# Clustered attention and a rational MoE layer on one core: the denominator's constant moves to ScalarE in three quarters of the units, under a new written-out order

## The chip, the core and the metric

The kernel runs on one core of a Trainium2 chip. The core has TensorE (PE in the profile), VectorE (DVE), ScalarE (ACT) and GpSimd (POOL) as compute engines and SyncE (SP), which issues the transfers here. Each engine works through its own list of instructions in order; between engines only semaphores order anything. The metric is the device time of one execution in microseconds (us), lower is better.

## What is computed

The reference, cut to what matters:

```python
# q, k, v: (4, 8, 768, 64); centroids: (8, 16, 64); w_in: (512, 2048); w_out: (2048, 512)
q_assign = argmax(einsum('bhsd,hcd->bhsc', q_n, c_n))      # the nearest of 16 centroids
k_assign = argmax(einsum('bhsd,hcd->bhsc', k_n, c_n))
mask = q_assign[:, :, :, None] == k_assign[:, :, None, :]
scores = where(mask, scale * q @ k^T, -1e9)
attn = exp(scores - max); attn = attn / (sum(attn) + 1e-9)
x = (attn @ v), heads put side by side: 3072 tokens x 512
h = x @ w_in
P = a[0] + a[1] * h + a[2] * h**2 + a[3] * h**3
Q = 1.0 + abs(b[0]) * abs(h) + abs(b[1]) * h**2
g = P / (Q + 1e-06)
out = g @ w_out
```

## The kernel before

The work is a batch's attention (four batches, four head pairs each), and behind it the batch's share of the MoE layer. The parts overlap: while the MoE of one batch runs, the attention of the next does. All products are made of float16 high and low parts, so a matrix product is three or four matmul passes.

**Attention.** For a head pair and a block of 128 queries, TensorE makes a tile of scores `s` (L987, four matmuls per head into one of two PSUM buffers named "s"). VectorE scales it and takes the extreme (L1016), ScalarE does the exponential and, with a tiny Copy, the sum's scale (`su`); VectorE inverts the sum (L1035); ScalarE writes the normalised high part `ah`, VectorE the low part (L1047), which is the last reader of the PSUM buffer. Then SP transposes `ah` to `at`, and TensorE multiplies by V (`px`, L1067). A batch-0 variant with keys first has lines from L1111 to L1225. L390 is the line of a helper through which nearly all ScalarE instructions go, so the names of the tiles tell them apart.

**MoE.** The work falls into 96 units: 4 batches x 3 blocks of 256 tokens x 4 blocks of the 2048 inner columns (`ci`) x 2 halves (`h`). A unit is a tile of 128 x 512. TensorE makes `ph` (the h of the reference; L1274, 24 matmuls, into one of two PSUM buffers named "m"); ScalarE reads it into `u` (absolute value) and `t` (start of the cubic); VectorE carries the cubic on (L1291, L1292, the last readers of `ph`). GpSimd completes the square of the denominator (L1336, L1337: s = u * (u + constant), so that Q = s + `cq`). ScalarE takes Ln of Q and Exp of its negative, which makes `u` about 1/Q. Then s becomes (s + cq) * u, t becomes (t + a0) * u (GpSimd L1365 and L1366, or VectorE L1372), and VectorE joins them in one Newton step (L1377). ScalarE casts the result to float16 (L1381), GpSimd or VectorE makes the low part (L1385), and TensorE multiplies by `w_out` into `po` (L1396, 12 matmuls of 128 x 512 per unit, six for each of its two blocks of 128 rows).

The constant `cq` can be added in two ways, and `acq`, a share between 0 and 1 spread evenly over the units, says in which:

```python
                acq = kshare("acq", b, i_)
                if acq:
                    act((724, 1165)[k], sv, sv, AF.Identity, [], ss, uu + kb("ln", b), [s_t], bias=cq)
                act((630, 1070)[k] if acq else (724, 1165)[k], uv, sv, AF.Ln, ss, us, uu + kb("ln", b), [s_t, u_t], **({} if acq else {"bias": cq}))
```

With `acq`, ScalarE adds it once in an Identity of its own, and Ln and the product (L1359) take s as it is. Without it, Ln takes cq as its bias, and GpSimd adds cq to s once more (L1354) ahead of the product L1359. In the last batch (`ed.3` is 1) VectorE makes the product (L1348) and adds the constant in the same instruction, so there is no L1354 there, with or without `acq`; the halves h = 1 of that batch use tiles named `sq1`, `sq2` and `sk1`, so that ScalarE's rows there read sq<-sq.

**Order.** The kernel writes some 4,200 steps into a list, and ORDER, a table of numbers, says in which order they are emitted; nothing reorders them behind it. So ORDER alone sets what stands where in each engine's list. The first number of each step's call (724 and so on) is not used.

Of the kernel before, what the change touches and what calls it, by code (L numbers as in the profile page):

```python
# [9 lines left out]
F32 = mybir.dt.float32  # L10
F32R = mybir.dt.float32r
F16 = mybir.dt.float16
BF16 = mybir.dt.bfloat16
# [5 lines left out]
P = 128  # L19
# [38 lines left out]
K = {'mulp': 0.6, 'mulp.3': 0.0, 'a0t': 1.15, 'xn': 14, 'scp': 1, 'vsc': 0.75, 'sup0': 0, 'stk': 2, 'lop': 0, 'mgp': 0, 'rvn': 2, 'at': 3, 'vn': 3, 'ah': 5, 'sqd': 0.0, 'ed': 0.0, 'ed.3': 1.0, 'gld': 0.0, 'gld.3': 1.0, 'sqd.3': 0.0, 'ghd': 0.0, 'sua': 1.0, 'acq': 0.4}  # L58
# [188 lines left out]
def clustered_attention_moe_kernel(  # L247
# [82 lines left out]

    plan.look = kn("look", 40.0)
    NM = 2
    NR = kn("NR", 12)

    def misc(shape, dt, name):
        return bank(shape, dt, "m", name, NM)
# [1149 lines left out]
```

## Time and profile before

| | |
|---|---|
| median of 3 runs | 958.12 us (957.24 to 958.2) |
| the profiled execution's own time | 954.15 us |
| its span in the trace | 952.3 us |
| mean granted TensorE clock | 0.993 |
| TensorE busy | 865.9 us |
| VectorE busy | 859.5 us |
| ScalarE busy | 802.1 us |
| GpSimd busy | 765.1 us |

The span is the time from the first to the last recorded instruction of the profiled execution; the time of that execution has 1.85 us more around it. Busy is the time in which an engine had at least one instruction in work; a matmul's end is modelled, so a busy TensorE need not be at its peak.

### The profile page before, as it was taken

To read this page: it belongs to the slowest core of one execution; us is meant where nothing else is said; L and a number is where in the kernel's file an instruction comes from. 1 tells how busy PE (TensorE), PEld (TensorE's weight loads), DVE (VectorE), ACT (ScalarE), POOL (GpSimd) and SP (SyncE) were. 2 spreads that over 40 slices of the span, in tenths; PEclk is the share of its full clock that TensorE was granted. 3 is DMA by queue.
4 is the path that set the end of the run, shared out by engine and by line. 5 is a ranking of instruction groups with operands and counts; after the bars stand their busy time and mean duration, and the time that the engine had idled before them with its cause. 6 is when DMAs were issued, how large, how long until landed. Compare 5 with 4: busy or idle time off the path is not lost.

```text
span 952.3 us, 20719 instructions
## 1 busy us (share of the span) xinstructions
PE 865.9 (91%) x7705; PEld 580.6 (61%) x7705; DVE 859.5 (90%) x1522; ACT 802.1 (84%) x1524; POOL 765.1 (80%) x801
## 2 busy tenths in 40 slices
PE   1679997988999998999989999999999999999997
PEld 1347665665666665656656666575576665766763
DVE  6888899778979999999999999999999998899986
ACT  5476786999989999889899999999899898876763
POOL 3557788899989899999998999998999998254452
PEclk9979999999999999999999999999999999999999
DMA  7994866797957779696879789696977667502000
GB/s 213 236 225 128 181 170 164 179 206 163 180 100 128 158 130 219 119 174 108 170 133 180 129 146 202 119 171 105 172 152 147 97 131 142 106 2 56 1 23 22
DMA packets 358932, 132.98 MB, mean 140 GB/s; under 512 B 335280, under 2 KB 351664, under 8 KB 358832
## 3 DMA queue, kind: packets, MB, share of 16 engines
q1 hardware_dynamic: 358832, 131.67, 68.8%
q8 instruction: 60, 0.98, 0.4%
q14 instruction: 40, 0.33, 0.1%
HBM read 41.98 MB, written 6.29 MB: 51 GB/s over the span
## 4 chain that ended last, share of the span: by engine, by line
PE 37%; DVE 32%; ACT 13%; issue 8%; DMA 6%; POOL 4%; SPq 0%; ACTq 0%; DVEq 0%; POOLq 0%
PE ph L1274 13%; PE po L1396 11%; DVE s L1016 6%; DVE ah L1047 5%; PE s L987 4%; PE px L1067 3%; DVE t L1377 3%; ACT s L390 3%; DMA rwi<-in_moe_w_in_dram 3%; DVE t L1291 2%; ACT u L390 2%; ACT ah L390 2%; DVE t L1292 2%; DVE top L1120 2%; DMA sq<-tq 2%
## 5 line engine op out<-in xcount | busy, mean ns | idle before, releaser
L1274 PE MATMUL ph<-x,win 128*128 128x256 f16 x2304 | 270.6, 273 | 3.7 <-DVE t L1292 3.1
L1274 PEld LDWEIGHTS <-win 128*128 128x128 f16 x2304 | 223.9, 98 | 49.4 <-DVE t L1292 5.9
L1396 PE MATMUL po<-wout,s 128*128 128x512 f16 x1008 | 239.5, 380 | 0.9 <-POOL s L1385 0.5
L1396 PEld LDWEIGHTS <-s 128*128 128x128 f16 x1008 | 96.5, 98 | 104.5 <-issue 4.6
L1016 DVE TENSOR_SCALAR_CACHE_REDUCE s<-s,cc 128x768 f32<-128x768 f32 x144 | 145.5, 1016 | 11.7 <-PE s L987 11.0
L1047 DVE SCALAR_TENSOR_TENSOR ah<-s,su,ah 128x768 f16<-128x768 f32 x144 | 144.7, 1009 | 7.4 <-ACT ah L390 6.6
L390 ACT ACTIVATE ah<-s,su 128x768 f16<-128x768 f32 x144 | 129.0, 899 | 18.0 <-DVE su L1035 17.1
L390 ACT ACTIVATE s<-s,nm 128x768 f32<-128x768 f32 x144 | 125.7, 873 | 12.5 <-DVE s L1016 11.1
L987 PE MATMUL s<-sk,sq 128*128 128x384 f16 x576 | 116.8, 327 | 19.6 <-DVE ah L1047 17.9
L1337 POOL TENSOR_TENSOR s<-s,u 128x512 f32<-128x512 f32 x84 | 113.9, 1356 | 7.0
L1359 POOL TENSOR_TENSOR s<-s,u 128x512 f32<-128x512 f32 x72 | 98.8, 1376 | 3.3 <-ACT u L390 3.1
L1385 POOL TENSOR_TENSOR s<-t,s 128x512 f16<-128x512 f32 x72 | 88.8, 1234 | 12.4 <-ACT s L1381 12.1
L1336 POOL TENSOR_SCALAR s<-u,g 128x512 f32<-128x512 f32 x84 | 77.2, 919 | 23.0 <-ACT u L390 21.7
L1377 DVE SCALAR_TENSOR_TENSOR t<-s,t 128x512 f32<-128x512 f32 x84 | 91.6, 1090 | 2.7 <-POOL s L1359 2.4
L987 PEld LDWEIGHTS <-sq 128*128 128x128 f16 x576 | 50.4, 98 | 67.6 <-DVE ah L1047 37.2
L1067 PE MATMUL px<-at,vhi 128*64 128x256 f16 x864 | 75.8, 277 | 4.3 <-DVE t L1292 4.1
L390 ACT ACTIVATE u<-ph,gk 128x512 f32<-128x512 f32 x84 | 57.4, 684 | 15.7 <-PE ph L1274 15.5
L1292 DVE SCALAR_TENSOR_TENSOR t<-t,gk,ph 128x512 f32<-128x512 f32 x84 | 62.8, 748 | 3.0
L390 ACT ACTIVATE t<-ph,gk 128x512 f32<-128x512 f32 x84 | 65.1, 777 | 0.0
L1291 DVE SCALAR_TENSOR_TENSOR t<-ph,gk,t 128x512 f32<-128x512 f32 x84 | 62.2, 740 | 1.0 <-ACT t L390 0.7
L1067 PE MATMUL px<-at,vlo 128*64 128x256 f16 x432 | 60.7, 275 | 0.0
L1366 POOL TENSOR_TENSOR t<-t,u 128x512 f32<-128x512 f32 x43 | 56.6, 1317 | 4.1 <-ACT u L390 0.6
(225 smaller groups left out, 1773.6 us busy)
## 6 DMA issues: line engine op xcount, KB each, us to landing
rwi<-in_moe_w_in_dram SPq DMA_DIRECT2D x16, 512.0 KB, 4.5
rwo<-in_moe_w_out_dram SPq DMA_DIRECT2D x16, 512.0 KB, 4.1
rk<-in_k_dram SPq DMA_DIRECT2D x32, 192.0 KB, 3.1
rq<-in_q_dram SPq DMA_DIRECT2D x32, 192.0 KB, 3.4
rvm<-in_v_dram SPq DMA_DIRECT2D x16, 384.0 KB, 4.0
rv<-in_v_dram SPq DMA_DIRECT2D x16, 384.0 KB, 4.4
out_dram<-ob SPq DMA_DIRECT2D x24, 256.0 KB, 3.0
at<-ah SPq DMA_TRANSPOSE x144, 4.1
```

The source lines that it names most:

```text
L390: lambda: nc.scalar.activation(out=out(), in_=in_(), func=func, **{a: (x() if callable(x) else x) for a, x in kw.items()}),
L987: nc.tensor.matmul(sc.ap[:, i, :SH], lhsT=st["q" + x].ap[:, j, t, :], rhs=st["k" + x].ap[:, j, ks, :].rearrange("p t c -> p (t c)"), start ...
L1016: lambda nm=nm, view=view: ts(out=view(), in0=view(), scalar1=cc.ap[:, 0:1], scalar2=None, op0=ALU.mult, op1=ALU.min, accum_out=nm.ap),
L1047: lambda part=part, view=view, su=su: stt(out=part(1), in0=view(), scalar=su.ap, in1=part(0), op0=ALU.mult, op1=ALU.subtract),
L1067: nc.tensor.matmul(px.ap[j * D : (j + 1) * D, :], lhsT=vv.ap[:, j, kt, :], rhs=at[j].ap[:, p_, kt].rearrange("p t c -> p (t c)"), start=(i ...
L1274: nc.tensor.matmul(ph.ap[:, fi * TW : (fi + 1) * TW], lhsT=win[:, wpart, c, f * P : (f + 1) * P], rhs=xs[c].ap[:, xpart], start=(i == 0), ...
L1292: stt(out=t[h].ap, in0=t[h].ap, scalar=col("a1")(), in1=ph.ap, op0=ALU.add, op1=ALU.mult)
L1337: nc.gpsimd.tensor_tensor(out=sv(), in0=sv(), in1=uv(), op=ALU.mult)
L1359: lambda uv=uv, sv=sv: nc.gpsimd.tensor_tensor(out=sv(), in0=sv(), in1=uv(), op=ALU.mult),
L1377: lambda tv=tv, sv=sv: stt(out=tv(), in0=sv(), scalar=2.0, in1=tv(), op0=ALU.subtract, op1=ALU.mult),
L1385: lambda tv=tv, g16=g16, e=(nc.vector if kshare("gld", b, i_) else nc.gpsimd): e.tensor_tensor(out=g16(1), in0=tv(), in1=g16(0), op=ALU.su ...
L1396: nc.tensor.matmul(po[ti].ap, lhsT=g16(gg)[:, c0 : c0 + P], rhs=wout[:, wpart, f, :], start=(i == 0 and f == 0), stop=(i == 2 and f == NF ...
```

## The change

The share `acq` goes from 0.4 to 0.75, and ORDER is written anew. Over the 96 units the Identity on ScalarE is there 72 times and not 38. In the first three batches that is 54 of 72 units and not 28: 26 units lose the GpSimd addition L1354 (44 before, 18 after) and get an Identity, and their Ln loses its bias. In the last batch it is 18 of 24 and not 10: 8 units get an Identity, and there is no GpSimd addition to lose. No other engine gains or loses a compute instruction (TensorE's, VectorE's lists hold as many rows as before).

```diff
-K = {'mulp': 0.6, 'mulp.3': 0.0, 'a0t': 1.15, 'xn': 14, 'scp': 1, 'vsc': 0.75, 'sup0': 0, 'stk': 2, 'lop': 0, 'mgp': 0, 'rvn': 2, 'at': 3, 'vn': 3, 'ah': 5, 'sqd': 0.0, 'ed': 0.0, 'ed.3': 1.0, 'gld': 0.0, 'gld.3': 1.0, 'sqd.3': 0.0, 'ghd': 0.0, 'sua': 1.0, 'acq': 0.4}
+K = {'mulp': 0.6, 'mulp.3': 0.0, 'a0t': 1.15, 'xn': 14, 'scp': 1, 'vsc': 0.75, 'sup0': 0, 'stk': 2, 'lop': 0, 'mgp': 0, 'rvn': 2, 'at': 3, 'vn': 3, 'ah': 5, 'sqd': 0.0, 'ed': 0.0, 'ed.3': 1.0, 'gld': 0.0, 'gld.3': 1.0, 'sqd.3': 0.0, 'ghd': 0.0, 'sua': 1.0, 'acq': 0.75}
...
 ORDER = [int(i) for i in """
-3 376 377 28 374 4 5 375 6 7 40 8 9 379 381 10 29 382 383 32 30 388 31 391 380 34 392 44 384 41 385 489 393
...
+3 377 376 28 374 4 5 375 6 7 40 8 9 379 381 29 382 383 32 30 10 388 31 391 380 34 33 392 44 384 41 385 398 489
...
-    NR = kn("NR", 12)
+    NR = kn("NR", 12 if kn("gw", 1) == 1 else 6)
...
+    def weights_wide(name, i, vt):
...
-                weights("wi", i, kn(f"wi{i}", -24 + 2.5 * i))
-                weights("wo", i, kn(f"wo{i}", -22 + 2 * i))
+                (weights_wide if GW == 2 else weights)("wi", i, kn(f"wi{i}", -24 + 2.5 * i))
+                (weights_wide if GW == 2 else weights)("wo", i, kn(f"wo{i}", -22 + 2 * i))
```

K has neither "gw" nor "c3" in it, so GW stays 1: the new function weights_wide is never called, NR stays 12, and the edit of a claim list (`tiles[: 3 if kn("c3") else 2]`) makes the same list as before. The new function shifts the lines behind it by 121: L1354 of before is L1475 of after.

What the new order does is seen in three places.

TensorE, around 361 us of the profiled execution: the last two score tiles of head pair 2 of batch 1 (`s1_2_5_0`, `s1_2_5_1`) and the first of head pair 3 (`s1_3_0_0`), which takes the PSUM buffer of `s1_2_5_0`. The first rows of each set, before:

```order
L987 MATMUL s1_2_5_0_5086<-sk11_2_3515,sq11_2_3542 128x384
...
L987 MATMUL s1_2_5_1_5098<-sk11_2_3515,sq11_2_3542 128x384
...
L1067 MATMUL px1_2_1_5119<-at1_2_1_0_4827,vhi1_2_3795 64x256
...
L987 MATMUL s1_3_0_0_5176<-sk11_3_4354,sq11_3_4378 128x384
```

and after:

```order
L1108 MATMUL s1_2_5_0_5074<-sk11_2_3521,sq11_2_3543 128x384
...
L1517 MATMUL po0_2_5083<-wout_104,s0_2_0_0_4741 128x512
...
L1108 MATMUL s1_2_5_1_5099<-sk11_2_3521,sq11_2_3543 128x384
...
L1517 MATMUL po0_2_5083<-wout_104,s0_2_0_0_4741 128x512
...
L1188 MATMUL px1_2_1_5124<-at1_2_1_0_4809,vhi1_2_3976 64x256
...
L1108 MATMUL s1_3_0_0_5178<-sk11_3_4355,sq11_3_4409 128x384
```

Each set of `po` left out here is of 6 matmuls and that of `px` of 36, in both lists. Two sets of `po` have come in between `s1_2_5_0` and `s1_3_0_0`, where before only the other score tile and the `px` stood.

ScalarE, at the MoE's first units (batch 0, block 0, ci 0): `u0_0_0_1`, `t0_0_0_1` and `s0_0_0_1` are the tiles of the half h = 1. Before:

```order
L390 ACTIVATE ah1_0_1_1_3057<-s1_0_1_1_2955,su1_0_1_1_3004 128x768
L390 ACTIVATE u0_0_0_0_2981<-u0_0_0_0_2981 128x512
L390 ACTIVATE rvm2_3_2934,vm2_2805<-rvm2_3_2934 128x768
L390 ACTIVATE u0_0_0_1_3008<-s0_0_0_1_3050,cq_76 128x512
L390 ACTIVATE u0_0_1_0_3096<-ph0_0_1_0_3011,gk0_2320 128x512
L390 ACTIVATE u0_0_0_1_3008<-u0_0_0_1_3008 128x512
```

and after:

```order
L390 ACTIVATE s0_0_0_1_3043<-s0_0_0_1_3043,cq_76 128x512
L390 ACTIVATE ah1_0_2_0_3131<-s1_0_2_0_3037,su1_0_2_0_3083 128x768
L390 ACTIVATE u0_0_0_1_3013<-s0_0_0_1_3043 128x512
L390 ACTIVATE u0_0_1_1_3153<-ph0_0_1_1_3087,gk0_2323 128x512
L390 ACTIVATE u0_0_0_1_3013<-u0_0_0_1_3013 128x512
```

The Identity `s0_0_0_1<-s0_0_0_1,cq` is new, and the Ln behind it (`u0_0_0_1<-s0_0_0_1`) has no bias; an `ah` of the attention stands between the two.

ScalarE, at the very end: the last unit is `ph3_2_3_1`, with its tiles `sq1`, `sk1` and `sq2`. Before:

```order
L390 ACTIVATE sk13_2_3_13059<-ph3_2_3_1_13000,gk3_8995 128x512
L1381 CAST s3_2_3_0_12956<-t3_2_3_0_12966 128x512
L390 ACTIVATE sq13_2_3_13045<-sq23_2_3_13054,cq_76 128x512
L390 ACTIVATE sq13_2_3_13045<-sq13_2_3_13045 128x512
L1381 CAST sq23_2_3_13054<-sk13_2_3_13059 128x512
```

and after:

```order
L1502 CAST s3_2_3_0_12958<-t3_2_3_0_12981 128x512
L390 ACTIVATE sq23_2_3_13063<-sq23_2_3_13063,cq_76 128x512
L390 ACTIVATE sq13_2_3_13043<-sq23_2_3_13063 128x512
L390 ACTIVATE sq13_2_3_13043<-sq13_2_3_13043 128x512
L1502 CAST sq23_2_3_13063<-sk13_2_3_13046 128x512
```

The last unit is one of those that get the Identity. In TensorE's list the last `ph` of this unit is followed by 54 matmuls of `po` before and by 60 after.

Elsewhere the new order keeps the stages and their sequence (the same head pair of attention stands beside the same block of the MoE), and moves single steps by a few places. At the start of the program the load `rv0_1` (384 KB) stands ahead of the transposes of `sk2` and `sq2` of head pair 0 and not behind them, and one preparation step of `w_in` on GpSimd (L555) is earlier.

## Rows read from the trace of the kernel before

**Rows 1.** The page, part 1: busy us, share of span, instructions:
```profile
PE 865.9 (91%) x7705; PEld 580.6 (61%) x7705; DVE 859.5 (90%) x1522; ACT 802.1 (84%) x1524; POOL 765.1 (80%) x801
```

**Rows 2.** Windows: length, busy us of each engine, clock, DMA:
```profile
180.00:780.00 600.00, 565.08 (x4983) 378.85 (x4983) 560.63 (x1018) 555.92 (x1088) 558.56 (x588) 1.00 0.80 150
780.00:953.00 173.00, 165.38 (x1193) 106.55 (x1192) 149.16 (x214) 121.64 (x212) 85.31 (x70) 1.00 0.25 50
```

**Rows 3.** The page, part 4: the chain by engine and line:
```profile
PE 37%; DVE 32%; ACT 13%; issue 8%; DMA 6%; POOL 4%; SPq 0%; ACTq 0%; DVEq 0%; POOLq 0%
PE ph L1274 13%; PE po L1396 11%; DVE s L1016 6%; DVE ah L1047 5%; PE s L987 4%; PE px L1067 3%; DVE t L1377 3%; ACT s L390 3%; DMA rwi<-in_moe_w_in_dram 3%; DVE t L1291 2%; ACT u L390 2%; ACT ah L390 2%; DVE t L1292 2%; DVE top L1120 2%; DMA sq<-tq 2%
```

**Rows 4.** The view of waits: us in total, times, longest:
```profile
PEld L987 <- DVE ah L1047: 37.2, 55, 1.9
...
PE s L987 <- DVE ah L1047: 17.9, 31, 1.4
```

**Rows 5.** Groups by form, the edited instructions: busy, mean ns:
```profile
L390 ACT ACTIVATE u<-s,cq 128x512 f32<-128x512 f32 x50 | 36.1, 722 | 3.7 <-POOL s L1337 3.6
...
L1354 POOL TENSOR_SCALAR s<-s,cq 128x512 f32<-128x512 f32 x44 | 34.5, 786 | 3.9 <-ACT su L390 1.6 <-ACT u L390 1.6
...
L390 ACT ACTIVATE s<-s,cq 128x512 f32<-128x512 f32 x34 | 24.4, 717 | 6.6 <-POOL s L1337 6.6
...
L390 ACT ACTIVATE u<-s 128x512 f32<-128x512 f32 x34 | 21.3, 626 | 0.2
```

**Rows 6.** One line (L1354): min/median/max ns, first and last start:
```profile
L1354 POOL TENSOR_SCALAR s<-s,cq x44: 686/695/1230, 217.9 to 797.1; 128x512 f32<-128x512 f32 x44
```

**Rows 7.** Groups by form, VectorE in the MoE part:
```profile
L1377 DVE SCALAR_TENSOR_TENSOR t<-s,t 128x512 f32<-128x512 f32 x84 | 91.6, 1090 | 2.7 <-POOL s L1359 2.4
...
L1292 DVE SCALAR_TENSOR_TENSOR t<-t,gk,ph 128x512 f32<-128x512 f32 x84 | 62.8, 748 | 3.0
...
L1372 DVE SCALAR_TENSOR_TENSOR t<-t,gk,u 128x512 f32<-128x512 f32 x41 | 44.8, 1092 | 0.1
...
L1372 DVE SCALAR_TENSOR_TENSOR sk<-sk,gk,sq 128x512 f32<-128x512 f32 x12 | 9.1, 760 | 0.3
...
L1377 DVE SCALAR_TENSOR_TENSOR sk<-sq,sk 128x512 f32<-128x512 f32 x12 | 8.6, 720 | 0.3
```

**Rows 8.** Timeline of TensorE: start, duration, instruction, idle before:
```profile
361.32 0.81 PE L987 MATMUL s<-sk,sq 128*128 128x384 f16 x4
362.38 0.82 PE L987 MATMUL s<-sk,sq 128*128 128x384 f16 x4 [0.24 <-DVE ah L1047]
364.76 0.41 PE L1067 MATMUL px<-at,vhi 128*64 128x256 f16 x4 [1.55 <-DVE t L1292]
...
368.20 0.82 PE L987 MATMUL s<-sk,sq 128*128 128x384 f16 x4 [1.29 <-DVE ah L1047]
```

**Rows 9.** Chain from 180 to 780 us: start, us, work:
```profile
243.17 2.59 PE po L1396 x12
...
245.76 2.10 PE px L1067 x36
```

**Rows 10.** Windows, 840 to 900 us:
```profile
840.00:900.00 60.00, 59.95 (x441) 41.03 (x440) 57.42 (x76) 42.14 (x71) 28.69 (x24) 1.00 0.12 23
```

**Rows 11.** Timeline of all engines at the end:
```profile
933.40 1.47 PE L1274 MATMUL ph<-x,win 128*128 128x256 f16 x12
...
939.54 0.72 ACT L390 ACTIVATE sq<-sq,cq 128x512 f32<-128x512 f32 x1 [0.34 <-POOL sq L1337]
...
944.18 0.62 ACT L1381 CAST sq<-sk 128x512 f16<-128x512 f32 x1 [3.26 <-DVE sk L1377]
...
944.88 3.04 PE L1396 MATMUL po<-wout,sq 128*128 128x512 f16 x12
```

**Rows 12.** Windows, 220 to 240 us:
```profile
220.00:240.00 20.00, 17.84 (x142) 11.62 (x141) 17.08 (x32) 19.69 (x40) 19.00 (x17) 1.00 0.83 179
```

More of the change, by code (lines that the diff above doesn't have):

```diff
@@ L627, in weights, with high, low, squares @@
                 )
+    def weights_wide(name, i, vt):
+        ew = wie if name == "wi" else woe
+        acc = buf([P, 1], F32, "acc", f"{name}a{i}", 2)
+        junk = temp([P, P], f"{name}j{i}")
+        ws = [buf([P, GW, FW], I32, "ring", f"w{name}{i}_{q}", NR) for q in range(2)]
+        for q, w in enumerate(ws):
+            halves = [half(w, h) for h in range(2)]
+            mag = wide(f"m{name}{i}_{q}")
+            mags = [half(mag, h) for h in range(2)]
+            raws = []
+            for h in range(2):
+                c = 2 * q + h
+                n = f"{name}{i}_{c}"
+                if name == "wi":
+                    src = moe_w_in[c * P : (c + 1) * P, i * FW : (i + 1) * FW]
+                else:
+                    src = moe_w_out[(4 * i + c) * P : (4 * i + c + 1) * P, :]
+                raw = buf([P, 2 * FW], I32, "wraw", "r" + n, 2)
+                raws.append(raw)
+                dma(1460, lambda raw=raw: raw.ap, lambda src=src: src.bitcast(I32), [], [raw], vt - kn("wd", 3))
+                def high(raw=raw):
+                    return raw.ap.rearrange("p (f two) -> p two f", two=2)[:, 1, :]
+                act(
+                    668, lambda mags=mags, h=h: mags[h].ap, lambda high=high: high().bitcast(F32), AF.Copy, [raw], [mags[h]], vt, [mag],
+                    scale=2.0 ** -112,
+                )
+            dve(
+                1050,
+                lambda w=w, mag=mag: nc.vector.tensor_single_scalar(
+                    out=w.ap, in_=mag.ap.bitcast(I32), scalar=3, op=ALU.logical_shift_left
+                ),
+                mags, halves, vt, [w, mag], n=1,
+            )
+            for h, raw in enumerate(raws):
+                def low(raw=raw):
+                    return raw.ap.rearrange("p (f two) -> p two f", two=2)[:, 0, :]
+                def high(raw=raw):
+                    return raw.ap.rearrange("p (f two) -> p two f", two=2)[:, 1, :]
+                dve(
+                    930,
+                    lambda w=w, h=h, low=low: stt(
+                        out=w.ap[:, h], in0=low(), scalar=29, in1=w.ap[:, h], op0=ALU.logical_shift_right, op1=ALU.bitwise_or
+                    ),
+                    [raw], [halves[h]], vt, [w], n=1,
+                )
+                act(
+                    668, lambda mags=mags, h=h: mags[h].ap, lambda high=high: high().bitcast(F32), AF.Sign, [raw], [mags[h]], vt, [mag],
+                )
+            op(
+                "POOL", 2300,
+                lambda w=w, mag=mag: nc.gpsimd.tensor_tensor(
+                    out=w.ap.bitcast(F32), in0=w.ap.bitcast(F32), in1=mag.ap, op=ALU.mult
+                ),
+                [*mags, *halves], [w], vt, [mag],
+            )
+        gram = misc([P, P], F32, f"{name}g{i}")
+        def squares():
+            blocks = [
+                w.ap.rearrange("p h c -> p (h c)").bitcast(BF16).rearrange("p (n two) -> p two n", two=2)[:, 1, m * P : (m + 1) * P]
+                for w in ws for m in range(2 * FW // P)
+            ]
+            for m, x in enumerate(blocks):
+                nc.tensor.matmul(gram.ap, lhsT=x, rhs=x, start=(m == 0), stop=(m == len(blocks) - 1))
+        op("PE", 1640, squares, ws, [gram], vt, [acc, junk])
+        dve(
+            360,
+            lambda: stt(
+                out=junk.ap, in0=gram.ap, scalar=1.0, in1=ident, op0=ALU.mult, op1=ALU.mult, accum_out=acc.ap
+            ),
+            [gram], [acc, junk], vt,
+        )
+        pn = misc([P, 1], F32, f"{name}n{i}")
+        def total():
+            nc.tensor.matmul(pn.ap, lhsT=ones, rhs=acc.ap, start=True, stop=True)
+        op("PE", 250, total, [acc], [pn], vt)
+        s = wsc[name]
+        we = Buf(None, None, 0, False)
+        whl[name, i, "e"] = we
+        ws_ = Buf(None, None, 0, False)
+        root_pow2(
+            pn, f"{name}p{i}", vt, lambda: ew.ap[:, i : i + 1], [ew, we], lambda: s.ap[:, i : i + 1], [ws_]
+        )
+        for q, w in enumerate(ws):
+            hl = [whl[name, i, 2 * q + h] for h in range(2)]
+            def part(j, q=q):
+                if name == "wi":
+                    return win[:, j, 2 * q : 2 * q + 2, i * FW : (i + 1) * FW]
+                return wout[:, j, 4 * i + 2 * q : 4 * i + 2 * q + 2, :]
+            def wf(w=w):
+                return w.ap.bitcast(F32)
+            act(
+                1160, lambda part=part: part(0), wf, AF.Identity, [w, ws_], hl, vt,
+                scale=lambda: s.ap[:, i : i + 1],
+            )
+            op(
+                "POOL", 1240,
+                lambda wf=wf: nc.gpsimd.tensor_scalar(
+                    out=wf(), in0=wf(), scalar1=s.ap[:, i : i + 1], scalar2=0.0, op0=ALU.mult, op1=ALU.add
+                ),
+                [ws_], [w], vt,
+            )
+            op(
+                "POOL", 2100,
+                lambda part=part, wf=wf: nc.gpsimd.tensor_tensor(out=part(1), in0=wf(), in1=part(0), op=ALU.subtract),
+                [w], hl, vt,
+            )
@@ L1282, in moe @@
                 for fi in range(2):
-                    op("PE", 12 * 108, lambda fi=fi, first=first: first(fi), [*xs, *wi, *wo, gk], [ph], u_ + h + kb("ph", b), tiles[:2], chain="ph")
+                    op("PE", 12 * 108, lambda fi=fi, first=first: first(fi), [*xs, *wi, *wo, gk], [ph], u_ + h + kb("ph", b), tiles[: 3 if kn("c3") else 2], chain="ph")
                 act(688, lambda u=u, h=h: u[h].ap, lambda ph=ph: ph.ap, AF.Abs, [ph, gk], [u[h]], u_ + h + kb("phr", b), [u_t], scale=col("kap"))
```

360 rows, old and new, of the table ORDER are left out of this document.

## The prediction

> **What bounds the kernel now.** I read the busy times first. Over the whole span TensorE is busy 91%, VectorE 90%, ScalarE 84%, GpSimd 80% [rows 1]: nobody has much room, and an average over stages hides which engine sets the pace where. So the span is cut in three [rows 2]. From 180 to 780 us, where attention of one batch and MoE of another run together, the four are within ten microseconds of each other: TensorE 565.1, VectorE 560.6, GpSimd 558.6, ScalarE 555.9 of 600. The reader should see four engines at 93 to 94%, none at 100: they wait for one another in turn, and TensorE idles 600 - 565.1 = 35 us. From 780 us on it is another picture: TensorE 165.4 of 173, ScalarE only 121.6, GpSimd 85.3. There TensorE alone is the bound.
>
> The chain that ended last agrees [rows 3]: 37% TensorE, 32% VectorE, 13% ScalarE, 4% GpSimd. A microsecond of work is not worth the same on every engine. ScalarE has 0.13 x 952.3 = 124 us on the chain out of 802.1 busy, which is 0.154 us of chain for each us of work; VectorE 305 of 859.5, 0.355; GpSimd 38 of 765.1, 0.05. These shares are my exchange rates for spread-out edits. They are local (a chain bends when work is added), so each has bounds beside it.
>
> The view of waits says what TensorE waits for: scores wait for VectorE's L1047, the last reader of the PSUM buffer they need, 37.2 us in 55 places at the weight loads and 17.9 in 31 at the matmuls [rows 4]. The two sums are of two queues that overlap in part, so they exceed the 35 us that TensorE really idled.
>
> **The change, part by part.** The profiled execution took 954.15 us (span 952.3, 1.85 around it), about 4 us under the median of 958.12. The sum is made against the former and then set on the median.
>
> *ScalarE.* A unit with the Identity costs 717 (Identity) + 626 (Ln without bias) - 722 (Ln with bias) = 621 ns more [rows 5]. In the first three batches 26 units change: 26 x 0.621 = 16.1 us. At 0.154 that is **+2.5 us**. Bounds: 0, if all of it falls into ScalarE's 44 us of idle time in that stretch; +16.1, if all of it is on the path. The 8 units of the last batch cost 8 x 0.621 = 5.0 us in a stretch where ScalarE idles 51 of 173 us: nothing, but for the last unit, which is counted under the tail.
>
> *GpSimd.* 26 of the 44 instructions L1354 go, at 786 ns: 20.4 us [rows 5]. All 44 lie between 217.9 and 797.1 us [rows 6], so the relief falls into the crowded stretch and none into the last one. At 0.05 it is **-1.0 us**; bounds 0 and -20.4.
>
> *VectorE, by way of GpSimd.* The instructions of VectorE that read two operands from SBUF are slower where GpSimd is busy. L1377 takes 1090 ns in its form with t (84 of them, over all stretches) and 720 in the form with sk (12, all in the last batch); L1372 1092 (41) against 760 (12). L1292, one operand of which is in PSUM, takes 748 in the same crowded stretch [rows 7]. The excess is 84 x 0.370 + 41 x 0.332 = 44.7 us. If it goes with GpSimd's busy time, 20.4 of 765.1 us less frees 1.2 us of VectorE; if it goes with GpSimd's busy share (93.1% in the middle, 49.3% at the end [rows 2]: 370 ns for 43.8 points, and 20.4 of 600 us is 3.4 points), it frees 29 ns on 125 instructions, 3.6 us. At 0.355: -0.4 to -1.3; I take the middle, **-0.9**.
>
> The Trainium skill has a harsher rule for this pair ("SBUF — State Buffer", section "Who interferes with whom"): a VectorE instruction with two SBUF inputs contends with a GpSimd instruction that reads SBUF, and the later one waits until the earlier has ended. The stretched 1090 and the unstretched 748 agree with which instructions it concerns. By it every dropped L1354 would hand VectorE its whole length, which is the fourth rival below.
>
> *The order, scores.* Two PSUM buffers serve the scores, so TensorE can make a tile only when the tile two before has been read by L1047. At 361 us the buffer of one tile is written until 361.32 + 0.81 = 362.13 and taken again at 368.20, after 1.29 us of waiting: the way round took 6.1 us [rows 8]. In between the old order gives TensorE only the other tile (0.82) and 36 `px` (2.10 us [rows 9]), 2.9 us of work, and TensorE waited 1.55 and 1.29 there. The new order puts two sets of six `po` in, 1.30 us each [rows 9]: 5.5 us. I counted this distance for all 142 pairs of the row-wise attention in both orders, with these durations. Under 6 us: 16 pairs, 11.7 us short in total before, 13 pairs, 9.4 after. Under 5 us: 3.2 short before, 1.4 after. So 1.8 to 2.3 us of waits fall away: **-2.0**, with 0 as the other bound, where the engines ahead of L1047 are late anyhow.
>
> *The tail.* From 840 to 900 us TensorE is busy 59.95 of 60 us [rows 10], so when the last `ph` comes is set by how much TensorE has ahead of it. The new order puts six `po` matmuls behind it that stood ahead: 1.30 us earlier [rows 9]. Behind it comes a chain of one unit through ScalarE, GpSimd and VectorE, from `ph` at 933.40 to the last `po` at 944.88, with Ln at 939.54 and the cast at 944.18 [rows 11]; ScalarE has waited 3.26 us ahead of that cast, so nothing else sets it. The new Identity adds 0.62 to this chain. Net **-0.7**; bounds -1.3 and +0.6. In the first three batches the same 0.62 is hidden: this chain, 10.0 us from the end of the last `ph` (933.40 + 1.47) to 944.88, is the only one I have to measure it by, and both orders leave TensorE at least 13 us of other work between a unit's `ph` and its `po`. Where a unit had no such cover, it would cost its 0.62.
>
> *The start.* The load of V for head pair 1 moves ahead of two transposes, and one weight step moves forward. No row prices it. I take 0.
>
> Sum: 2.5 - 1.0 - 0.9 - 2.0 - 0.7 = -2.1 us. 954.15 becomes 952.0, and the median 958.1 becomes **956.0**.
>
> **The rivals.**
>
> *A, the balance above:* 956.0, its own range 951 to 961 (the Identities at twice their exchange rate, or at none; the order's terms at 0 or as they stand).
>
> *B, the order gives more than I can count.* The 35 us that TensorE idles in the middle come from many places; I counted one kind. For it: scores waiting on L1047 are the largest wait in the view [rows 4]. Against it: the milestones of the two orders are alike, and steps moved only by some places. A quarter of the 35 us, 8.8: about 949.
>
> *C, the other side: ScalarE becomes the bound.* In the middle stretch it goes from 555.9 to 572.0 us, above TensorE's 565.1. The busiest engine there now runs at 565.1 / 600 = 94.2%. If ScalarE can do no better, the stretch becomes 572.0 / 0.942 = 607 us, +7.3; with the tail's -0.7 that gives about 964.5. It decides once ScalarE has gained over 9.2 us, 15 of the 26 units. For it: behind the first MoE units ScalarE is busy 19.69 of 20 us already [rows 12], so it can be full, and everything that TensorE waits for (exponential, `ah`, `u`) goes through it. Against it: only 13% of the chain is its own, and at 19.69 of 20 it shows that it can run well above 94%.
>
> *D, the shared access is the true bound.* If each dropped L1354 hands VectorE its 695 ns [rows 6], 26 of them are 18.1 us, all of them worth it if VectorE set the pace: 940. Against it: the mean stretch is 370, not 695 ns, and VectorE has a third of the chain.
>
> *E, nothing happens:* each engine's terms are absorbed by its neighbours' idle time, 958.
>
> **How the numbers follow.** About 0.2%, 1.9 us, is what a measurement of this kernel can tell from no change. Chances: A 0.50, B 0.15, C 0.22, D 0.05, E 0.08. The point is A's 956.0, 2.1 us under the median, so A itself is split: about half of it faster by more than 1.9 us, a third within, the rest slower. Faster: 0.26 of A with B and D, 0.46. Same: 0.18 of A with E, 0.26. Slower: 0.06 of A with C, 0.28. The range, 947 to 965, takes in A and E, most of B, and the nearer half of C; it leaves out D, B's far end and C's worse half, some 2 in 10.
>
> **What the profile after would show.** L1354, now L1475, 18 times, and ScalarE's busy time near 802.1 + 16.1 + 5.0 = 823, GpSimd's near 745: else the counts are wrong. The means of L1377 and L1372 in their forms with t some 10 to 30 ns lower: if 100 or more, D is at work. Waits of scores for L1047 some 2 us less, and no 1.29 ahead of `s1_3_0_0`. At the end the last `ph` starts about 1.3 us earlier in relation to TensorE's work, and the way from there to the last `po` is 0.6 longer. If ScalarE shows over 96% from 180 to 780 us and TensorE's waits on ScalarE's tiles grow by more than those on L1047 shrink, C was right and the exchange rate of 0.154 is the step that failed. A start that is later by more than a microsecond would make the forecast wrong with none of these steps at fault.

## The result: 12.7 us faster, where 2.1 were forecast

| | before | after |
|---|---|---|
| median of 4 runs | 958.16 us | 945.46 us (943.42 to 947.64) |
| ratio | 1 | 0.9868 (95%: 0.9838 to 0.9897) |
| profiled execution, span | 954.15, 952.3 us | 947.64, 945.9 us |

The ratio's interval is a gain of 9.9 to 15.5 us. The direction was right; the size was six times too small and the time lies below the range (947 to 965). The two profiled executions differ by only 6.5 us: that of before lies under all four runs of its row and had a mean granted TensorE clock of 0.993, that of after is the slowest of its four and had 0.987. So stages are compared by work done in a stretch, not by span alone.

The page of the changed kernel, part 1 (busy us of each engine) and part 4 (the chain):

```profile
PE 868.2 (92%) x7705; PEld 584.7 (62%) x7705; DVE 857.7 (91%) x1522; ACT 814.1 (86%) x1558; POOL 743.2 (79%) x775
...
PE 42%; DVE 27%; ACT 15%; issue 8%; DMA 6%; POOL 2%; SPq 1%; ACTq 0%; DVEq 0%; POOLq 0%
```

Against [rows 1, 3] GpSimd is down by 22 us, ScalarE up by 12, TensorE and VectorE as they were: the same work in less time. VectorE's share of the chain fell from 32% to 27%, TensorE's rose from 37% to 42%. ScalarE was forecast near 823 us and shows 814.1, though it ran the 34 additional instructions. Busy time counts once what overlaps, and in this order more of ScalarE's work overlaps (see x3_identity_at_ln).

The windows of the changed kernel, columns as in [rows 2]:

```profile
180.00:780.00 600.00, 573.25 (x5065) 386.71 (x5064) 568.72 (x1030) 570.81 (x1131) 549.88 (x570) 1.00 0.80 152
780.00:946.00 166.00, 158.16 (x1123) 102.48 (x1121) 141.08 (x200) 118.76 (x205) 71.43 (x61) 0.99 0.23 46
```

In the same 600 us TensorE was busy 573.3 us and not 565.1, VectorE 568.7 and not 560.6, and ScalarE, which got the additional work, 570.8 and not 555.9. The middle of the program is denser on three engines at once; TensorE idles 26.8 us there and not 34.9. ScalarE stands at 95.1% there, above the 94.2% that I took for what an engine can reach.

The groups by form of the changed kernel, those that answer to [rows 5, 7]:

```profile
L1498 DVE SCALAR_TENSOR_TENSOR t<-s,t 128x512 f32<-128x512 f32 x84 | 85.8, 1022 | 0.1
...
L1493 DVE SCALAR_TENSOR_TENSOR t<-t,gk,u 128x512 f32<-128x512 f32 x41 | 46.4, 1131 | 0.2 <-ACT u L390 0.2
...
L390 ACT ACTIVATE s<-s,cq 128x512 f32<-128x512 f32 x60 | 43.5, 724 | 1.1 <-POOL s L1458 1.1
...
L1475 POOL TENSOR_SCALAR s<-s,cq 128x512 f32<-128x512 f32 x18 | 15.3, 850 | 0.5 <-ACT su L390 0.2
```

The counts are as forecast: 18 additions on GpSimd, 60 Identities of this form (12 more on the sq tiles). L1498, which was L1377, came down by 68 ns; L1493, which was L1372, went up by 39; together 4.1 us less VectorE work.

### The profile page after: what moved, and what is told of

Read it like the earlier page. It is cut to its first block, busy times and chain, and to the rows that moved or that the text cites. A ratio compares the mean times of both kernels' runs of the same rounds, so it can differ in the third digit from the quotient of the medians.

```text
span 945.9 us, 20726 instructions
## 1 busy us (share of the span) xinstructions
PE 868.2 (92%) x7705; PEld 584.7 (62%) x7705; DVE 857.7 (91%) x1522; ACT 814.1 (86%) x1558; POOL 743.2 (79%) x775
## 4 chain that ended last, share of the span: by engine, by line
PE 42%; DVE 27%; ACT 15%; issue 8%; DMA 6%; POOL 2%; SPq 1%; ACTq 0%; DVEq 0%; POOLq 0%
PE ph L1395 14%; PE po L1517 13%; DVE s L1137 6%; DVE ah L1168 5%; PE s L1108 5%; ACT s L390 3%; PE px L1188 3%; DVE t L1498 2%; ACT ah L390 2%; DVE t L1412 2%; DMA rwi<-in_moe_w_in_dram 2%; ACT u L390 2%; DVE t L1413 2%; PE s L1232 2%; PE z L1276 2%
## 5 line engine op out<-in xcount | busy, mean ns | idle before, releaser
L1457 POOL TENSOR_SCALAR s<-u,g 128x512 f32<-128x512 f32 x84 | 76.0, 905 | 37.3 <-ACT u L390 31.9
L1498 DVE SCALAR_TENSOR_TENSOR t<-s,t 128x512 f32<-128x512 f32 x84 | 85.8, 1022 | 0.1
```

The source lines that it names most:

```text
L1498: lambda tv=tv, sv=sv: stt(out=tv(), in0=sv(), scalar=2.0, in1=tv(), op0=ALU.subtract, op1=ALU.mult),
```

## The experiments

Times are medians; each ratio is to the kernel before in runs on the same chip, with its 95% interval. The first run below, e1_old_order_acq75, is the order of before with the share 0.75. Its order and the new one differ by 462 exchanges of neighbours (two steps that follow each other in an engine's list change places) on TensorE, 1798 on ScalarE, 1062 on VectorE, 633 on GpSimd and 566 on SP; no TensorE step moves by more than ten places.

### The edit without the order, the order without the edit

The steps that one order has and the other lacks are tied to a neighbour: an Identity directly ahead of its Ln, an addition directly ahead of its product. For the first run (`was` is the share for which the order was written):

```diff
-                if acq:
-                    act((724, 1165)[k], sv, sv, AF.Identity, [], ss, uu + kb("ln", b), [s_t], bias=cq)
+                if was:
+                    op("ACT", 724, plus if acq else (lambda: None), [], ss)
...
+                def ln(uv=uv, sv=sv, plus=plus, put=acq and not was, bias=not acq):
+                    if put:
+                        plus()
+                    nc.scalar.activation(out=uv(), in_=sv(), func=AF.Ln, **({"bias": cq} if bias else {}))
```

**e1_old_order_acq75.** 

> The order of before with the share 0.75: the Identity is put directly ahead of its Ln, the additions L1354 that the change drops are dropped, nothing else moves. If the new order made the gain (theory O: fewer waits of scores and of TensorE by where the steps stand), this is near before, 956 to 960 us. If the edit made it (theory R: GpSimd's 20 us less work and what VectorE gets back of it), this is near the changed kernel, 944 to 949. By my exchange rates (2.5 - 1.0 - 0.9 and the tail's 0.6) it would be 959.

Measured: 962.02 us, 1.0040 (1.0024 to 1.0057).

**e2_new_order_acq40.** 

> The new order with the share 0.4: the additions on GpSimd are put back directly ahead of their product, the Identities go. Theory O: near the changed kernel, 943 to 948 us. Theory R: near before, 955 to 959. If both are needed (the new order was made for the other split of work and fits only that), it is slower than both single effects would give, and the first run is slower than before too.

Measured: 953.11 us, 0.9946 (0.9927 to 0.9965), between the two theories. So:

| | order of before | new order | the order is worth |
|---|---|---|---|
| share 0.4 | 1 | 0.9946 | -5 us |
| share 0.75 | 1.0040 | 0.9868 | -16 us |
| the edit is worth | +4 us | -7 us | |

Neither theory holds alone: the edit costs time under the old order and saves time under the new one. By themselves the edit and the order make +3.8 and -5.2 us, together -1.4; with both it is -12.7. Some 11 us (7 to 15, from the three intervals) come only when the new order and the new share are together. A hint at why is in the chains (part 4 of the two pages), first of the order of before with 0.75:

```profile
PE 35%; DVE 28%; ACT 18%; issue 8%; DMA 6%; POOL 4%; SPq 0%; ACTq 0%; DVEq 0%; POOLq 0%
```

then of the new order with 0.4:

```profile
PE 33%; DVE 26%; POOL 17%; ACT 10%; issue 8%; DMA 5%; POOLq 0%; SPq 0%; ACTq 0%; DVEq 0%
```

Under the old order the Identities put ScalarE on the chain with 18%, and before it was 13% [rows 3]. Under the new order and the old share GpSimd has 17% of the chain; in the changed kernel it has 2%. So with the other split one engine takes a larger part of the chain than in either kernel. That this is the cause is argued, not shown: shares of the chain turn out below to be poor prices. And part of the 11 us may lie in where these two runs put the steps that their order lacks, directly beside a neighbour.

### The two halves of the edit, each alone

**e3_drop_adds_only** leaves out the addition L1354 in all but 18 units (the edit is given in short; `acq_new` is the share of the changed kernel, `acq_old` that of before):

```diff
-                    if not acq: op(
+                    if not acq_new: op(
```

> The order of before, its Identities as before (38), but only 18 of the 44 additions L1354, as in the changed kernel: the constant is left out of the product or of the join in some units and is in it twice in others. GpSimd loses 20.4 us, ScalarE gains nothing. By my rates -1.9 us (956); by theory R -10 or more (948 or less); by the harshest count, each dropped addition handed on whole, -18 (940). Theory O says nothing beyond the -1.9.

Measured: 958.60 us, 1.0009 (0.9989 to 1.0030). GpSimd's 20 us are worth 1.1 us at most here (0.05 for each), not 18: rival D is out for this order.

**e4_identities_only** takes the Identities by the new share and keeps the 44 additions:

```diff
-                if acq:
+                if acq_new:
...
-                    if not acq: op(
+                    if not acq_old: op(
```

> The order of before, the Identities as in the changed kernel (72 and not 38), the additions L1354 as before (44): the constant is in the product twice in some units. ScalarE gains 16.1 us in the first three batches and 5.0 in the last. By my rates +2.5 and 0.6 at the tail (961 us); if ScalarE is the bound of the middle, as rival C had it, +6 to +16 (964 to 974); if ScalarE has room, 958.

Measured: 964.72 us, 1.0075 (1.0053 to 1.0097): 7 us for 21 us of ScalarE work, 0.34 us for each (0.24 to 0.44), where I took 0.154.

The two halves do not add up either. From this run to the first one the same 26 additions go, now beside the new Identities, and the time falls by 0.35% (0.08 to 0.63), where e3 showed nothing. Under the new order neither half was run alone.

### Less work on VectorE and on TensorE

```diff
-                    stt(out=t[h].ap, in0=ph.ap, scalar=col("rho")(), in1=t[h].ap, op0=ALU.mult, op1=ALU.mult)
+                    n = 512 if last else 296
+                    stt(out=t[h].ap[:, :n], in0=ph.ap[:, :n], scalar=col("rho")(), in1=t[h].ap[:, :n], op0=ALU.mult, op1=ALU.mult)
```

**v_less.** 

> The kernel before, with VectorE's first step of the cubic (L1291) on 296 of its 512 columns in the 72 units of the first three batches; the cubic's other columns miss that step. By 216 of 512 columns of 740 ns it loses some 0.22 to 0.31 us each, 16 to 22 us of VectorE, all of it among the crowded stretch. Theory V (VectorE sets the pace there: in every trace so far the stretch from the first to the last score tile is 572 to 576 us plus VectorE's idle time): most of it comes off the time, 946 or less. By my exchange rate of 0.355, 6 to 8 us, 950. If TensorE sets the pace, or the engines' fit alone, nothing or slower: 957 or more.

Measured: 953.35 us, 0.9956 (0.9938 to 0.9973). The shortened instruction took 515 ns, so VectorE lost 72 x 0.226 = 16.3 us, and the kernel 4.2: 0.26 for each (0.16 to 0.36), which takes in the 0.355 of the chain and is far from 1. VectorE does not set the pace alone.

```diff
                         for wpart, xpart in ((0, 0), (0, 1), (1, 0)):
+                            if i == 11 and not last:
+                                break
                             nc.tensor.matmul(
...
-                                start=(i == 0), stop=(i == 3 * NCC - 1),
+                                start=(i == 0), stop=(i == 3 * NCC - (1 if last else 2)),
```

**p_less.** 

> The kernel before, without the last of the 12 matmuls that make each half of ph in the first three batches (one product of parts is missing from the sum): 144 x 0.109 = 15.7 us less work for TensorE, spread as in the run with less VectorE work. If TensorE sets the pace, 945; by its rate on the chain (0.37 x 952.3 / 865.9 = 0.41), 952; by theory V 956 or more, since TensorE would only wait longer for VectorE.

Measured: 957.18 us, 1.0003 (0.9986 to 1.0020). Its windows:

```profile
180.00:780.00 600.00, 556.25 (x4824) 367.11 (x4824) 556.82 (x1015) 554.31 (x1086) 556.79 (x584) 0.99 0.79 149
```

TensorE is busy 8.8 us less in the stretch and idles 8.8 us more; VectorE and ScalarE get through as many instructions as before (1015 and 1086 against 1018 and 1088 in [rows 2]). Over the whole program its busy time is 861.0 us and not 865.9: only 4.9 of the 15.7 us show, as the matmuls that are left took longer in this execution, whose mean granted clock was 0.982 and not 0.993. By the times alone a microsecond of this engine, with the largest share of the chain, is worth 0.09 at most. The 12 runs had a mean clock of 0.982 and the 17 of the kernel before beside them 0.984, which may hide another 1.5 us (by the estimate at the end of the experiments).

### One engine's sequence from the new order

Here and below the fences tell in words how the table ORDER was made, which is all that these runs change. Steps are emitted by position, as soon as what they read is written and a buffer is free. Share 0.75; E is the engine of the run. A tile takes its place among the rotating buffers at the first step that uses it, so the sequence in which buffers are taken changes with the order, too.

```diff
-position(step) = place in the order of before
+position(step) = place in the new order if step.engine == E else place in the order of before
```

**h_pe.** 

> The share 0.75 and the order of before (962.0 us on its own against 958.5), with the new order's sequence on TensorE alone; the other engines keep the old one but for a few places that the dependences force. If the gain of 16.6 us from the order is TensorE's own (theory P: matmuls of other work put between the score tiles, so that it waits less), most of it shows here: 950 or less. If it lies in how the other engines' steps stand, 960 to 963. My own term for the scores would give 960.

 Measured: 1051.37 us, 1.0983 (1.0953 to 1.1013).

**h_act.** 

> The share 0.75 and the order of before, with the new order's sequence on ScalarE alone. Theory S: what costs is where the Identities and Ln stand among the exponentials and the high parts of the attention; in the new order 57 of the 72 Identities have other work between them and their Ln, in the first run only 19. Then most of the gain shows here: 952 or less. By theory P, 960 to 963.

 Measured: 1080.04 us, 1.1283 (1.1253 to 1.1312).

**h_dve.** 

> The share 0.75 and the order of before, with the new order's sequence on VectorE alone. Theory V: VectorE's steps L1047 and L1016, for which scores and exponentials wait, stand earlier than the MoE's steps; then 952 or less. By theories P and S, 960 to 963. If the gain is in no engine's sequence alone but in their fit, each of these single runs is near 962 or even slower.

 Measured: 1045.26 us, 1.0910 (1.0881 to 1.0939).

**h_poolsp.** 

> The share 0.75 and the order of before, with the new order's sequence on GpSimd and on SP, which issues the transfers. GpSimd has 2% of the chain of the changed kernel, so by all three theories above 960 to 963; if transfers (the early load of V, the transposes) matter, up to 5 us less, and the difference shows in the first 180 us.

 Measured: 1007.39 us, 1.0513 (1.0484 to 1.0541).

All four lie far above every figure written down for them; only h_dve's text had "or even slower". They do not tell which engine's sequence makes the gain, since breaking the fit costs much more than the 16 us in question. The waits of h_act show the form of it:

```profile
PEld L1107 <- DVE ah L1167: 60.7, 56, 4.6
POOL s L1456 <- ACT u L389: 53.4, 21, 7.8
POOL s L1505 <- ACT s L1501: 51.7, 20, 5.7
POOL sq L1456 <- ACT sq L389: 50.7, 7, 14.1
PE s L1107 <- DVE ah L1167: 48.1, 48, 4.1
ACT s L389 <- DVE s L1136: 42.0, 38, 3.6
```

With ScalarE's list from one order and the others' from the other, TensorE, VectorE, ScalarE and GpSimd wait for one another, for up to 4 to 14 us at a time. An order of this kernel is one object; by such exchanges its engines' lists cannot be judged apart.

### Where ScalarE's steps stand

**x2_ah_first** moves `su` or `ah` ahead of the steps directly before it in ScalarE's list, nearly all of the MoE, in 15 places of the first run's order (18 exchanges):

```diff
-position(ah) = place in the first run's order
+position(ah) = position(the MoE step that it stood behind) - 0.5
```

> The share 0.75 and the order of before (962.0 on its own), with ScalarE's su or ah put ahead of the MoE's ScalarE steps directly before it in 15 places, those where the trace showed VectorE waiting for it while it stood ready behind such a step; these waits sum to 5.7 us. Nothing else moves. If VectorE's waits for ScalarE's attention steps are what the order repairs (theory V), 956 to 959. If any single displacement upsets the fit, 962 or more.

Measured: 964.70 us, 1.0079 (1.0058 to 1.0100), no gain on the first run's 1.0040 but 0.4% more (0.1 to 0.7). The waits did not go away either. From 180 to 780 us:

```profile
DVE ah L1168 <- ACT ah L390: 8.9, 18, 1.3
...
DVE su L1156 <- ACT su L390: 7.4, 14, 1.9
```

That is 16.3 us against 18.0 in the first run (its rows are below): of the 5.7 us that were aimed at, 1.7 went. So whether shorter waits of this kind would have gained time, this run does not tell.

**x3_identity_at_ln** changes the position of the Identities alone:

```diff
-position(Identity) = place in the new order
+position(Identity) = position(its Ln) - 0.5
```

> The changed kernel with each of the 72 Identities put directly ahead of its Ln, as in the first run; 57 of them move back by one to nine places in ScalarE's list (132 exchanges of neighbours in all), nothing else does. If the places of the Identities carry the gain, 950 or more. If the rest of the order does, 944 to 947.

Measured: 949.40 us, 0.9912 (0.9895 to 0.9929), about 4 us behind the changed kernel's 0.9868; the intervals just touch, and the difference is 0.4% (0.1 to 0.8). The waits from 180 to 780 us, in the changed kernel:

```profile
PEld L1108 <- DVE ah L1168: 22.9, 38, 1.7
...
PE s L1108 <- DVE ah L1168: 15.3, 26, 1.3
...
ACT ah L390 <- DVE su L1156: 7.3, 19, 0.8
DVE s L1137 <- PE s L1108: 6.8, 19, 0.8
...
DVE su L1156 <- ACT su L390: 4.4, 12, 1.4
...
DVE ah L1168 <- ACT ah L390: 1.6, 5, 0.6
```

in this run:

```profile
PEld L1107 <- DVE ah L1167: 24.0, 44, 1.6
...
PE s L1107 <- DVE ah L1167: 14.3, 26, 1.5
...
DVE su L1155 <- ACT su L389: 9.8, 18, 2.3
...
DVE ah L1167 <- ACT ah L389: 4.7, 13, 0.6
```

in the first run, the order of before with 0.75:

```profile
PEld L987 <- DVE ah L1047: 31.8, 50, 1.9
...
PE s L987 <- DVE ah L1047: 16.3, 32, 1.4
...
ACT ah L390 <- DVE su L1035: 10.2, 22, 1.2
DVE s L1016 <- PE s L987: 9.8, 16, 2.1
DVE ah L1047 <- ACT ah L390: 9.2, 22, 1.3
...
DVE su L1035 <- ACT su L390: 8.8, 16, 1.9
```

and in the kernel before:

```profile
DVE su L1035 <- ACT su L390: 8.3, 15, 1.9
...
DVE ah L1047 <- ACT ah L390: 5.9, 10, 1.5
```

TensorE's wait for L1047 at its matmuls is the same in the first three, 14 to 16 us; at its weight loads (PEld) it is 31.8 us in the first run and 24.0 and 22.9 under the new order. VectorE's waits for ScalarE's `su` and `ah` are 18.0 us in the first run and 6.0 in the changed kernel; with the Identities put back at their Ln they are 14.5. So the Identities' places alone move 8.5 us of these waits, each sum read from one execution, and some 4 us of time (1 to 8). But these waits do not set the time by themselves: in the kernel before they are 14.2 us, as many as in this run, which is 8 us faster.

What the places do on ScalarE itself shows in its timeline. In this run an Identity and its Ln:

```profile
410.90 0.72 ACT L389 ACTIVATE s<-s,cq 128x512 f32<-128x512 f32 x1
411.65 0.63 ACT L389 ACTIVATE u<-s 128x512 f32<-128x512 f32 x1
```

and in the changed kernel an Identity with a step behind it that does not read its tile:

```profile
410.94 0.73 ACT L390 ACTIVATE s<-s,cq 128x512 f32<-128x512 f32 x1
411.56 0.77 ACT L390 ACTIVATE t<-ph,gk 128x512 f32<-128x512 f32 x1
```

The Ln, which reads what the Identity writes, starts 0.03 us after its end; a step that does not need it starts 0.11 before. In the means over the program it is 0.03 after (72 pairs in this run) and 0.10 before (52 places in the changed kernel, where 15 pairs are left). So 57 pairs at 0.13 us, 7 us by estimate, are what the places are worth on ScalarE; its busy time is 819.3 us here and 814.1 in the changed kernel. The first run, which puts the new Identities directly ahead of their Ln, has 53 such pairs and the kernel before 15. A part of the edit's price under the old order is of this kind; how much was not tried.

### The two orders joined at one place

All engines change over at the same step, the first that makes score tile n; share 0.75. For the first two runs (for the others the orders are swapped):

```diff
-position(step) = place in the order of before
+position(step) = place in the new order if it is ahead of tile n there, else behind all of these, by the order of before
```

**c_new48_old.** 

> The share 0.75; all engines in the new order up to the 49th of the 144 row-wise score tiles (422 us in the changed kernel), in the order of before behind it. Theory L (each stretch of the new order earns its own part, wherever the rest comes from): the changed kernel is 8.5 us ahead of the first run (order of before, share 0.75) at this tile, so 962.0 - 8.5 = 953.5, between 951 and 956. Theory F (the gain is in a fit of the whole list, and a seam costs as the exchanged single engines did): 960 or more.

 Measured: 951.69 us, 0.9953 (0.9934 to 0.9971).

**c_new96_old.** 

> The same with the seam at the 97th score tile (625 us in the changed kernel), where it is 11.8 us ahead of the first run. Theory L: 950, between 948 and 953. Theory F: 960 or more.

 Measured: 947.56 us, 0.9908 (0.9889 to 0.9928).

**c_old48_new.** 

> The share 0.75; the order of before up to the 49th score tile, the new one behind it. Theory L: what the run with the seam at the same place and the parts the other way round does not earn, 962.0 - 16.5 + 8.5 = 954, between 951 and 957. If all the gain is early, 962; theory F, 960 or more.

 Measured: 955.19 us, 0.9989 (0.9971 to 1.0008).

**c_old0_new.** 

> The share 0.75; the order of before up to the first row-wise score tile (the first 196 us: loads, weights, the keys-first attention of batch 0), the new one behind it. I took the start for nothing: then 944 to 947, as the changed kernel. In the profiles the new order comes to this tile 2 to 4 us later than the others; if that is lost time, 942 to 944. If the early load of V pays later, 948 or more.

 Measured: 945.76 us, 0.9896 (0.9874 to 0.9917).

By the ratios, from 1.0040 for the old order: the new one up to tile 49 earns 0.9%, up to tile 97 1.3%, the whole 1.7%; from tile 49 on alone 0.5%. 0.9 and 0.5 make 1.4, within the intervals (some 0.3 each) of the whole. So a seam costs little, the gain is spread over the middle, and theory F falls for seams across all engines; the four times lie in the ranges of theory L or, c_new96_old, 0.4 us under it. The traces agree: VectorE's step L1016 of the 49th tile starts at 422.34 us in the changed kernel,

```profile
422.34 1.02 DVE L1137 TENSOR_SCALAR_CACHE_REDUCE s<-s,cc 128x768 f32<-128x768 f32 x1
```

and at 430.80 in the first run:

```profile
430.80 1.02 DVE L1016 TENSOR_SCALAR_CACHE_REDUCE s<-s,cc 128x768 f32<-128x768 f32 x1
```

The start under either order gives the same time within the intervals.

That the first half earns more than the second is not shown, for the granted TensorE clock differed. It was 0.991 in the mean of c_new48_old's runs and 0.984 in those of c_old48_new. Within the runs of one kernel the time goes with it: of the 17 runs of the kernel before beside these, the four at 0.982 and 0.983 took 957.6 to 959.3 us, those at 0.991 and 0.993 took 953.3 and 953.0. From these I estimate 0.5 to 0.6 us for each thousandth, 3.5 to 4 us for the seven thousandths, and the two runs lie 3.5 us apart.

## Why the prediction was wrong, step by step

**The step that failed: the sum, which priced the edit and the order apart and added them.** For the order it has -2.0 ("So 1.8 to 2.3 us of waits fall away") and the -1.3 in "Net -0.7" of the tail, 3.3 us in all; for the edit +2.5 - 1.0 - 0.9 and the Identity's 0.6 in the tail, +1.2. Run alone, the order gave -5.2 (-3.4 to -7.0) and the edit +3.8 (2.3 to 5.5). Their sum, -1.4, is near the forecast of -2.1. What the sum had at nothing, without a reason, is that one is worth more with the other: 11 of the 12.7 us. With the share 0.75 the order is worth 1.0040 - 0.9868 = 1.7%, 16 us. I priced two places that I could count in a list and took the rest for neutral because the stages stand in the same sequence. The direction came out right, but not by these terms, which leave less than the 1.9 us that the prediction itself could not tell from no change.

**The scores.** The place was right and the use of it wrong. The changed kernel at this spot, TensorE's timeline:

```profile
360.54 0.82 PE L1108 MATMUL s<-sk,sq 128*128 128x384 f16 x4 [1.01 <-DVE ah L1168]
361.20 1.46 PE L1517 MATMUL po<-wout,s 128*128 128x512 f16 x6
362.50 0.81 PE L1108 MATMUL s<-sk,sq 128*128 128x384 f16 x4
363.15 1.46 PE L1517 MATMUL po<-wout,s 128*128 128x512 f16 x6
...
366.94 0.82 PE L1108 MATMUL s<-sk,sq 128*128 128x384 f16 x4 [0.25 <-DVE ah L1168]
```

The wait of 1.29 us in [rows 8] is 0.25, and the tile comes 6.4 us after the one two before it and not 6.9. The waits over the whole program:

```profile
PEld L1108 <- DVE ah L1168: 27.5, 41, 2.1
...
PE s L1108 <- DVE ah L1168: 18.6, 29, 1.9
```

Against [rows 4] the wait of the weight loads fell by 9.7 us, that of the matmuls did not fall (17.9 before). The two overlap in part, so neither is a gain of time. And TensorE's work was the wrong thing to price by the chain: p_less took some of it off, and that was worth little or nothing. The largest share of the chain belonged to an engine with slack.

**The exchange rates.** They took each engine's share of the chain as the worth of its work. Measured under the old order: ScalarE 0.34 where I took 0.154, VectorE 0.26 (0.16 to 0.36) for 0.355, GpSimd 0 (0.05 at most) for 0.05, TensorE 0 (0.09 at most by the times, some 0.2 if the clock hid 1.5 us) for 0.41 (used only in an expectation). So TensorE's rate and ScalarE's were off, the other two lie within what was measured. And they do not carry over to another order: the edit that costs 4 us under the old order saves 7 under the new one, where GpSimd had 17% of the chain without it. My +1.2 for the edit stands against +3.8 (2.3 to 5.5) in the first run.

**VectorE's relief.** Forecast 1.2 to 3.6 us of its work. In e3, which removes the additions and nothing else, L1377 and L1372 in their forms with t are 17 and 10 ns shorter, 1.8 us together: the size was right, and the kernel's time did not move. In the changed kernel they lost 4.1, but L1493 became longer, so that is not GpSimd's relief alone.

**The tail.** The end of the changed kernel:

```profile
926.97 1.47 PE L1395 MATMUL ph<-x,win 128*128 128x256 f16 x12
...
933.59 0.72 ACT L390 ACTIVATE sq<-sq,cq 128x512 f32<-128x512 f32 x1 [1.66 <-POOL sq L1458]
...
937.78 0.62 ACT L1502 CAST sq<-sk 128x512 f16<-128x512 f32 x1 [2.15 <-DVE sk L1498]
...
938.64 2.87 PE L1517 MATMUL po<-wout,sq 128*128 128x512 f16 x12
```

From the last `ph` to the last `po` it is 11.67 us, and was 11.48 [rows 11]: 0.2 more, not 0.62, since GpSimd's part of it was shorter (its first step, L1457, took 0.69 us here, and as L1336 1.51 before). The six matmuls behind the last `ph` no run tried alone.

**The start.** Taken as nothing. The first row-wise score tile reaches VectorE at 198.4 us in the changed kernel and at 194.3 in the kernel before, the later start of which the prediction warned. But c_old0_new, with the start of before, took 945.76 us, and its own trace has that tile at 198.0, so the start is not what failed.

**The rivals.** C's price was in the right range for the Identities alone (7 us in e4, which left the order as it was; its terms add up to 964.7 and not 964.5). Its point of decision was wrong: it took 94.2% for the most that an engine reaches, and under the new order ScalarE stands at 95.1% of the middle. Whether ScalarE sets the time there was not tried. B was the nearest, "the order gives more than I can count": it named a quarter of TensorE's idle time in the middle, 8.8 us, and that idle time fell by 8.2, though not at the matmuls that wait for L1047. But by e2 the order alone gives 5 us; the rest needs the new share.

**What stays open.** The Identities' places account for some 4 (1 to 8) of the order's 16 us. The rest is spread over the middle; in which engine's list it lies was not shown, and the rule that I tried (attention's steps first, x2) earned nothing. The pairs on ScalarE do not explain the rest: the first run has 178 places where a ScalarE step, waiting for no other engine, does not overlap the one before it, the changed kernel 109, and of these 69 the Identities' places make 54 (163 in x3). Nor was the granted clock held equal: 0.983 in the mean of the 23 runs of the kernel before beside e1 and e2, 0.985 in e1, 0.988 in e2 and in the changed kernel. At 0.5 to 0.6 us for each thousandth some 1 to 3 of the 12.7 us go with it, by estimate, and no run tells whether the clock is the cause there or follows from the order.

## What to carry to other kernels

Where four engines are all 93% busy, a share of the chain is not the worth of a microsecond: measure it by changing the work of one engine at a time a little, which under the old order gave about 0 for TensorE and GpSimd, 0.26 for VectorE and 0.34 for ScalarE. Such a price holds for the order and the split it was measured with. A written-out order and the split of work that it was made for belong together: run each alone before you add them. A new order must not be priced by the places that one happens to see; with such a diff the range has to be wide on both sides. To find where an order earns its time, join the two at a step that all engines share; exchanging one engine's list broke the fit here.

## What was not expected

Some 400 exchanges of neighbours in TensorE's list, where no step moved by more than ten places, cost 10%, and the four runs of this kind 5 to 13% (49 to 123 us). Leaving out 144 matmuls (15.7 us) of the engine that the page shows at 91% and with 37% of the chain changed the time by 0.03% (-0.14 to +0.20).

On ScalarE a step that reads what the step directly before it wrote costs 0.13 us more than one that does not (0.03 us after its end, where others start 0.10 before it). Moving 57 Identities away from the step that reads them went with some 4 us of the kernel's time.
